# Storing the gradients of two neighbouring heads as one transfer with 16 KiB rows, in the second pass of an attention backward kernel

## The chip, the cores and the metric

The kernel runs on one core of one Trainium2 chip. The metric is the device time of one execution in microseconds; the program does the whole computation, forward and backward, in one launch. A core has TensorE (PE; its weight loads are shown apart, as PEld), VectorE (DVE), ScalarE (ACT), GpSimd (POOL) and SyncE (SP), which run their own instruction streams in order and wait for each other by semaphores. Sixteen DMA engines move data between the main memory (HBM) and the on-chip memory (SBUF, 128 partitions). A transfer that SP issues goes through hardware queue q1; one that GpSimd issues goes through software queue q0.

## The reference

One decode step (one query per sequence, a cache of 4096 keys) of a block with attention and an MLP, and the gradients of all its inputs. What is computed for the cache, cut to what matters (B = 2 sequences, H = 32 heads, Sk = 4096, Dh = 128, all in bfloat16):

```python
q = (layernorm(x) @ wq).reshape(B, 1, H, Dh).transpose(0, 2, 1, 3)
scores = einsum("bhqd,bhkd->bhqk", q, k_cache) * (Dh ** -0.5)
p = softmax(scores)
o = einsum("bhqk,bhkd->bhqd", p, v_cache)
h = x + o.transpose(0, 2, 1, 3).reshape(B, 1, H * Dh) @ wo
out = h + relu(layernorm(h) @ w1) @ w2
# returned: out and the gradients of x, k_cache, v_cache, wq, wo, w1, w2
```

For one query the gradients of the caches are outer products. With `go` the gradient at `o` of a head, `dp = v_cache @ go` and `gs = p * (dp - dot)`, where `dot` is one number for each head: gV = p (outer) go and gK = gs (outer) q, each 4096 x 128 for every one of the 64 pairs (sequence, head). So 64 MB of keys and 64 MB of values are read, the values a second time in most cases, and 128 MB of gradients are written.

## The kernel before

**Layout.** A head's cache of 1 MB is one tile of 128 partitions: partition p holds the 32 neighbouring rows 32p to 32p+31, 8 KiB that are contiguous in HBM (`natural`, L498). A gradient tile has the same layout, so each 1 MB transfer has 128 rows of 8 KiB.

**First pass** (`p1_iter`, L508). It reads K and V of all 64 pairs in order and makes the probabilities P (kept in `P_bf`, L233) and what the middle needs. The middle (`middle_gen`, L860) gives `go` for groups of heads.

**Second pass** (`p2_iter`, L971). In the order `turns` (L455) it goes through the pairs once more. For pair j it reads V again (tile W; six of each sequence's V tiles are kept from the first pass), transposes it on TensorE in four groups (`pair_transpose`, L474: four transposes into PSUM tile t_ps, then ScalarE copies to t_sb) and multiplies with go (`pair_matvec`, L490) into `dp`. Two matmuls spread the rows go and q over all partitions of the same PSUM bank (L985), ScalarE scales them into `rb` (L990), and GpSimd doubles P into `pp` (L992; VectorE's outer product reads each factor twice side by side). VectorE makes the gV tile in two halves of 2048 elements (`outer_half`, L951). In the next turn `p2_gs` (L959) makes the scaled gradient `gsp`, doubled, from `dp`, and VectorE makes gK in two halves. Each tile is stored when its second half is there (L1004, L1025).

The plan (L1243 to L1249) starts the second pass beside the first: pairs 0 to 13 of it run there, and store through GpSimd. Pairs 14 to 63 and the last gK run alone (`i is None`), and store through SP. There ScalarE makes eight of a gV's 32 blocks (L1024, `act`) for pairs up to j = 32, with factors `pa` that GpSimd casts (L996). Work of the middle and of the end (`fin_gen`, L1106: the weight gradients `ot`, stored through GpSimd at L1101; `gx_gen`, L1140: the gradient of x) runs in between, by a given rate a step.

**Buffers.** Thirteen 1 MB homes in the pool `big` (8 KiB a partition) carry tags: `ld` for loads, `g` for gradient tiles, `f` for `ot`, `q` for the end's loads. `take` and `give` (L112, L128) hand them around first in, first out; `share` (L141) sets how many each tag should own. When the second pass is alone, a pool `big1` adds two homes and the shares are ld = 10, of which six hold kept V tiles, and g = 5. Later the six tiles of the weights wo come free one after the other (`late`, L1317), three for g and three for q. Loads wait in a list (`pump`, L1268) and are issued on SP, in the program's order with the stores, as soon as a home of `ld` is free; SP waits in that order.

Of the kernel before, what the change touches and what calls it, by code (L numbers as in the profile page):

```python
# [7 lines left out]
FP32 = mybir.dt.float32  # L8
BF16 = mybir.dt.bfloat16
ALU = mybir.AluOpType  # L10
# [5 lines left out]
def kernel(  # L16
# [89 lines left out]
    owned = dict(free)  # L106
    wanted = {}
    pools = [big] * NBIG
    home_of = {}
    given_at = {}  # L110

    def take(tag, shape, name):  # L112
        assert free[tag] > 0, (tag, name)
        free[tag] -= 1
        k = homes[tag].pop(0)
        t = pools[k].tile(shape, BF16, tag=tag_of.get(k, f"big{k}"), bufs=1, name=name)
        home_of[id(t)] = (tag, k, t)
        return t

    def goes_to(tag):  # L120

        if owned[tag] > wanted.get(tag, len(pools)):
            for other in homes:
                if owned[other] < wanted.get(other, 0):
                    return other
        return tag

    def give(t, to=None):  # L128
        tag, k, _ = home_of.pop(id(t))
        to = to or goes_to(tag)  # L130
        owned[tag] -= 1
        owned[to] += 1
        free[to] += 1
        homes[to].append(k)
        given_at[k] = step[0]
# [14 lines left out]
                    d[tag] -= 1  # L150
                    d[to] += 1

    tag_of = {}

    def more_home(tag, pool, name=None):
        if name:
            tag_of[len(pools)] = name
        homes[tag].append(len(pools))
        pools.append(pool)
        free[tag] += 1  # L160
        owned[tag] += 1
# [70 lines left out]
    NPS = 52  # L232
    P_bf = cols.tile([128, NPS, NSC], BF16)  # L233
    P_free = list(range(NPS))
    P_slot = {}
    ga = cols.tile([128, B, NF], FP32)
    nc.vector.memset(ga[:], 0.0)
# [127 lines left out]
    qc = pkp.tile([128, H, B], BF16)  # L365
    WH = 6
    NWO = -(-H // WH)
    wo_t = [wop.tile([128, NSC * 128], BF16, tag=f"wo{t}", bufs=1, name="wo_t") for t in range(NWO)]

    def wo_of(h, c0, c1):  # L370
        return wo_t[h // WH][:, (h % WH) * D + c0:(h % WH) * D + c1]
# [73 lines left out]
    pairs = [(b, h) for b in range(B) for h in range(H)]  # L445
    NP1 = len(pairs)
    KEPT = (6, 6)
    GROUPS = []
    for b in range(B):
        first = H - KEPT[b]  # L450
# [497 lines left out]
    def pairs_view(t):  # L948
        return t.rearrange("p s (a two) -> p s a two", two=2)

    def outer_half(dst, row, colp, k, short=0):  # L951
        n = HALF - short
        sl = slice(k * HALF, k * HALF + n)
        nc.vector.tensor_tensor(  # L954
            out=pairs_view(dst[:, sl, :]),
            in0=row.rearrange("p (a two) -> p a two", two=2)[:, None, :, :].to_broadcast([128, n, 64, 2]),
            in1=colp[:, sl, None, :].to_broadcast([128, n, 64, 2]), op=ALU.mult)
# [10 lines left out]
        P_free.append(P_slot.pop((bp, hp)))  # L968
        return gsp

    def p2_iter(j, busy, act=0, store=None):  # L971
        store = store or nc.gpsimd

        c = S2[j] if j < NP1 else None
        p = S2.get(j - 1)
        if p is not None:
            bp, hp = turns[j - 1]
            gsp = p2_gs(j - 1)
        if c is not None:
            b, h = turns[j]  # L980
            go = gom[:, h, b, :, :]

            bank = pst([128, 512], FP32, "sps", "dp_ps")
            for k, col in enumerate((goc, qsc)):
                nc.tensor.matmul(bank[:, 128 + k * 128:256 + k * 128],  # L985
                                 lhsT=col[:, h, b:b + 1].to_broadcast([128, 128]), rhs=ident_bf[:],
                                 start=True, stop=True)
            c["dp"] = bank[:, 0:NSC]
            rb = mats.tile([128, 256], BF16, tag="rb", bufs=3, name="rb")
            nc.scalar.activation(out=rb[:], in_=bank[:, 128:384], func=ACT.Copy, scale=rt[:, b, h:h + 1])  # L990
            pp = small.tile([128, NSC, 2], BF16, tag="pp", bufs=2, name="pp")
            nc.gpsimd.tensor_copy(out=pp[:], in_=P_bf[:, P_slot[(b, h)], :, None].to_broadcast([128, NSC, 2]))  # L992
            c.update(rb=rb, pp=pp)
            if act:
                pa = small.tile([128, act], FP32, tag="pa", bufs=2, name="pa")
                nc.gpsimd.tensor_copy(out=pa[:], in_=P_bf[:, P_slot[(b, h)], NSC - act:NSC])  # L996
            c["T0"] = pair_transpose(c["W"], 0, busy=busy)
        if p is not None:
            gK = take("g", [128, NSC, 128], "gK")
            outer_half(gK, p["rb"][:, 128:256], gsp, 0)  # L1000
        yield
        if p is not None:
            outer_half(gK, p["rb"][:, 128:256], gsp, 1)
            store.dma_start(out=natural(out_2, bp, hp), in_=gK[:])  # L1004
            give(gK)
            del S2[j - 1]
        yield
        if c is None:
            return
        c["T1"] = pair_transpose(c["W"], 1, busy=busy)  # L1010
        pair_matvec(c["dp"], c.pop("T0"), 0, go)
        yield
        c["T2"] = pair_transpose(c["W"], 2, busy=busy)
        pair_matvec(c["dp"], c.pop("T1"), 1, go)
        yield
        c["T3"] = pair_transpose(c["W"], 3, busy=busy)
        give(c["W"], "g" if j < H and j != 1 and owned["g"] < 3 else None)
        pair_matvec(c["dp"], c.pop("T2"), 2, go)
        gV = take("g", [128, NSC, 128], "gV")
        outer_half(gV, c["rb"][:, 0:128], c["pp"], 0)  # L1020
        yield
        outer_half(gV, c["rb"][:, 0:128], c["pp"], 1, act)
        for k in range(act):
            nc.scalar.activation(out=gV[:, NSC - act + k, :], in_=c["rb"][:, 0:128], func=ACT.Copy, scale=pa[:, k:k + 1])  # L1024
        store.dma_start(out=natural(out_3, b, h), in_=gV[:])  # L1025
        give(gV)
        yield


    def p2_tail(j):  # L1030

        p = S2[j]
        bp, hp = turns[j]
        gsp = p2_gs(j)
        yield
        gK = take("g", [128, NSC, 128], "gK")
        outer_half(gK, p["rb"][:, 128:256], gsp, 0)
        yield
        outer_half(gK, p["rb"][:, 128:256], gsp, 1)
        nc.gpsimd.dma_start(out=natural(out_2, bp, hp), in_=gK[:])  # L1040
        give(gK)
        del S2[j]
        yield
# [254 lines left out]
    def p2_step():  # L1298
        nonlocal g2
        try:  # L1300
            next(g2)
        except StopIteration:
            g2 = None

    for n, (i, j) in enumerate(plan):
        all_go = all(("go", B - 1, h) in done for h in range(H))
        if i is None and plan[n - 1][0] is not None:
            pkp.release()
            big1 = tc.alloc_tile_pool(name="big1", bufs=1)
            for _ in range(2):  # L1310
                more_home("ld", big1)
            share(ld=KEPT[1] + 4, g=5)
        if ("w1", B - 1) in done:
            for t in range(NWO):
                if t not in late and all(("go", B - 1, h) in done for h in range(t * WH, min(H, (t + 1) * WH))) and \
                        (t < NWO - 1 or all_go):
                    late[t] = ("g", "g", "g", "q", "q", "q")[len(late)]  # L1317
                    more_home(late[t], wop, f"wo{t}")
        lq, ll, lg = [sum(v == tag for v in late.values()) for tag in ("q", "ld", "g")]
        if fin is not None and not bg2 and not bg3:  # L1320
            share(ld=4, g=12 + 6 * (lq > 0))
        elif fin is not None and j >= H + KEPT[1] - 1:
            share(ld=4 + ll, g=7 + lg, f=3, q=2 + lq)
        if j is not None:
            while g2 is not None:
                p2_step()
            if j < NP1:
                bg_until(("go", *turns[j]))
            if i is not None and n + 1 < len(plan) and plan[n + 1][1] is None:
                g2 = p2_whole(j)  # L1330
            else:
                g2 = p2_iter(j, 0, 8 if i is None and j <= H else 0, nc.sync if i is None else None)
        if i is None and ("w1", 1) in done and fin is None:
            wts.release()
            fin = tc.alloc_tile_pool(name="fin", bufs=1)
            big2 = tc.alloc_tile_pool(name="big2", bufs=1)
            more_home("f", big2)
            banks.update(sps=[2, 3], o=[4, 5, 6])
            bg2.append(("fin", fin_gen(fin)))
            bg3.append(("gx", gx_gen(fin)))  # L1340
        if i == 12:
# [9 lines left out]
        if i is None:  # L1351
            mixed[0] = False
            spread[0] = 2
            at_k[0] = 1
            k = 0
            while g2 is not None:
                p2_step()
                pump()
                slot[0] = int(k in ((1, 3, 5) if j <= H else (1, 4)))
                k += 1  # L1360
                bg_step(0, rate)
                bg_step(1, RATE2 * (0.4 if spreading[0] else 1.0))
                bg_step(2, RATE3)
            continue
# [64 lines left out]
```

## Time and profile before

| | |
|---|---|
| median of three runs | 890.82 us (889.17 to 891.23) |
| profiled execution | 887.9 us |
| its span, first to last instruction | 886.1 us |
| busy: PE, PEld | 736.0 us, 614.3 us |
| busy: DVE, ACT, POOL | 690.8 us, 478.0 us, 155.8 us |
| moved by DMA | 361.87 MB, mean 408 GB/s over the span |
| second pass alone | from about 456 us to the end |
| last instruction of a compute engine | ends at about 868 us |

Engines work side by side, so the rows do not add up. A slice line of the profile divides the span into 40 equal slices and gives tenths of busy time; a stretch's row gives busy microseconds of each engine with the number of instructions, the clock that TensorE was granted, the mean share of the 16 DMA engines and what they moved. A wait row names the engine that waits, the line, who ended the wait, the total, the number of times and the longest. An issue row gives the number of transfers, their size and the median time from issue to landing.

### The profile page before, as it was taken

How to read it: one execution, taken by the hardware profiler on the slowest of the kernel's cores; microseconds unless marked ns; L12 is line 12 of the kernel's file. 1: busy time of each engine (PE TensorE's matmuls, PEld its weight loads, DVE VectorE, ACT ScalarE, POOL GpSimd, SP SyncE). 2: the span in 40 equal slices, each digit the busy share in tenths (PEclk: the TensorE clock that was granted, in tenths of full speed). 3: DMA queues.
4: the chain of work that ended last, by engine and by line, in shares of the span. 5: the costliest groups of instructions: out<-in, count | busy, mean ns of one | idle time of the engine just before them, and what ended most of it. 6: DMA issues, size and time to landing. Idle time of an engine off the chain costs nothing.

```text
span 886.1 us, 24945 instructions
## 1 busy us (share of the span) xinstructions
PE 736.0 (83%) x10215; PEld 614.3 (69%) x10215; DVE 690.8 (78%) x1309; ACT 478.0 (54%) x1241; POOL 155.8 (18%) x264
## 2 busy tenths in 40 slices
PE   4999899999999998878967777878878896937971
PEld 4888788888888887777856666656757665625640
DVE  2666698877888887777868797678989998799750
ACT  1344343344565655455546777767756555526661
POOL 1344344343210000010011110011010001101200
PEclk9999899999999999999996556555666756556565
DMA  9999999999889999999999999999999999999995
GB/s 377 425 417 417 421 413 420 424 423 416 323 298 392 424 424 426 423 424 426 423 405 415 422 425 425 425 422 412 419 425 414 419 419 427 415 426 421 408 425 229
DMA packets 56115, 361.87 MB, mean 408 GB/s; under 512 B 5712, under 2 KB 11728, under 8 KB 15296
## 3 DMA queue, kind: packets, MB, share of 16 engines
q1 hardware_dynamic: 49096, 317.04, 86.5%
q0 software_dynamic: 6864, 43.22, 11.7%
q8 instruction: 80, 1.31, 0.5%
q14 instruction: 35, 0.29, 0.1%
q10 hardware_dynamic: 40, 0.01, 0.0%
HBM read 211.11 MB, written 149.13 MB: 407 GB/s over the span
## 4 chain that ended last, share of the span: by engine, by line
PE 38%; DMA 21%; DVE 19%; issue 12%; ACT 8%; SPq 0%; POOL 0%; ACTq 0%; POOLq 0%; DVEq 0%
PE t_ps L482 17%; DMA Vt<-in_A_v_cache_dram 10%; PE m_ps L516 9%; DVE gK L954 5%; DVE gV L954 5%; DMA out_dram<-gK 4%; DVE rows L711 4%; DVE pk L523 3%; ACT t_sb L487 3%; PE s_ps L495 3%; PE u_ps L545 3%; DMA out_dram<-ot 2%; ACT gV L1024 2%; DMA wqs<-in_A_wq_dram 2%; PE dp_ps L495 2%
## 5 line engine op out<-in xcount | busy, mean ns | idle before, releaser
L487 ACT COPY t_sb<-t_ps 128x512 f32<-128x512 f32 x479 | 274.2, 587 | 208.7 <-PE t_ps L482 205.4
L495 PEld LDWEIGHTS <-t_sb 128*128 128x128 bf16 x4096 | 177.7, 102 | 57.2 <-ACT t_sb L487 28.8
L482 PE MATMUL t_ps<-ident_f,Wt 128*128 128x128 f32 x832 | 192.6, 381 | 9.0 <-DMA Wt<-in_A_v_cache_dram 8.4
L523 DVE TENSOR_TENSOR pk<-Kt,ep 128x2048 bf16<-128x2048 bf16 x128 | 156.3, 1222 | 39.7 <-ACT ep L570 31.4
L516 PE MATMUL m_ps<-pk,Vt 128*128 128x129 bf16 x2048 | 170.6, 222 | 13.5 <-DMA Vt<-in_A_v_cache_dram 13.5
L482 PEld LDWEIGHTS t_ps<-ident_f,Wt 128*128 128x128 f32 x832 | 134.7, 197 | 38.1 <-issue 30.6
L482 PE MATMUL t_ps<-ident_f,Kt 128*128 128x128 f32 x1024 | 157.0, 286 | 4.1 <-DMA Kt<-in_A_k_cache_dram 3.4
L954 DVE TENSOR_TENSOR gK<-rb,gsp 128x2048 bf16<-128x2048 bf16 x128 | 153.2, 1222 | 8.9 <-DMA out_dram<-gV 7.1
L516 PEld LDWEIGHTS <-Vt 128*128 128x128 bf16 x2048 | 124.5, 98 | 43.5 <-issue 27.7
L954 DVE TENSOR_TENSOR gV<-rb,pp 128x2048 bf16<-128x2048 bf16 (+1 forms) x128 | 143.3, 1140 | 2.7 <-DMA out_dram<-gK 2.6
L482 PEld LDWEIGHTS t_ps<-ident_f,Kt 128*128 128x128 f32 x1024 | 113.5, 145 | 7.8 <-ACT t_sb L487 3.8
L533 POOL COPY pk<-ep 128x16 bf16<-128x16 bf16 x78 | 83.2, 1069 | 155.6 <-ACT ep L570 80.5
L495 PE MATMUL dp_ps<-gom,t_sb 128*128 128x2 bf16 x2048 | 95.3, 168 | 16.9 <-ACT t_sb L487 16.0
L495 PE MATMUL s_ps<-qm,t_sb 128*128 128x2 bf16 x2048 | 87.6, 164 | 1.3 <-DVE t_sb L485 1.3
L1099 ACT CAST ot<-o_ps 128x512 bf16<-128x512 f32 (+3 forms) x152 | 66.8, 493 | 5.1 <-DMA out_dram<-ot 3.0
L992 POOL COPY pp<-P_bf 128x64 bf16<-128x64 bf16 x64 | 30.3, 478 | 163.6 <-DVE gV L954 152.0
L630 ACT CAST wo_t<-m_ps 128x128 bf16<-128x128 f32 x55 | 14.6, 266 | 78.1 <-PE m_ps L516 77.9
L711 DVE CUSTOM_DVE_ANT_0 rows<-wqs,gqr 128x1024 bf16<-128x1024 bf16 x40 | 48.9, 1221 | 9.6 <-DMA wqs<-in_A_wq_dram 9.4
L990 ACT ACTIVATE rb<-dp_ps,rt 128x256 bf16<-128x256 f32 x64 | 30.3, 473 | 44.2 <-PE dp_ps L985 43.3
L711 DVE CUSTOM_DVE_ANT_0 rows<-wo_t,rows 128x640 bf16<-128x640 bf16 x64 | 52.4, 819 | 0.8 <-ACT rows L688 0.4
L1024 ACT ACTIVATE gV<-rb,pa 128x128 bf16<-128x128 bf16 x152 | 46.5, 392 | 6.4 <-DMA out_dram<-gV 6.4
L711 DVE CUSTOM_DVE_ANT_0 rows<-w_t,rows 128x640 bf16<-128x640 bf16 (+2 forms) x53 | 42.3, 799 | 2.9 <-ACT rows L688 2.7
(205 smaller groups left out, 690.3 us busy)
## 6 DMA issues: line engine op xcount, KB each, us to landing
Kt<-in_A_k_cache_dram SPq DMA_DIRECT2D x64, 1024.0 KB, 18.7
Vt<-in_A_v_cache_dram SPq DMA_DIRECT2D x64, 1024.0 KB, 15.1
Wt<-in_A_v_cache_dram SPq DMA_DIRECT2D x52, 1024.0 KB, 16.4
out_dram<-gK SPq DMA_DIRECT2D x51, 1024.0 KB, 16.7
out_dram<-gV SPq DMA_DIRECT2D x50, 1024.0 KB, 15.1
out_dram<-gV POOLq DMA_DIRECT2D x14, 1024.0 KB, 10.4
out_dram<-gK POOLq DMA_DIRECT2D x13, 1024.0 KB, 10.3
out_dram<-ot POOLq DMA_DIRECT2D x6, 960.0 KB, 10.0
```

What stands on the lines that cost most here:

```text
L482: nc.tensor.transpose(t_ps[:, j, :], natf[:, 2 * cc:2 * cc + 2, :].rearrange("p c k -> p (c k)"), ident_f[:])
L487: nc.scalar.copy(out=t_sb[:], in_=t_ps[:])
L495: nc.tensor.matmul(dst[:, sc:sc + 2], lhsT=v[:, j, :, par], rhs=vecs[:, par, :], start=(par == 0), stop=(par == 1))
L516: nc.tensor.matmul(r["m"][:, 0:129], lhsT=r["V"][:, sc, :], rhs=r["pk"][sc // HALF][:, sc % HALF, 0:129], start=(sc == 0), stop=(sc == NSC ...
L523: nc.vector.tensor_tensor(out=p["pk"][k][:, :, 0:128].rearrange("p s (a two) -> p s a two", two=2), in0=p["K"][:, sl, :].rearrange("p s (a ...
L533: nc.gpsimd.tensor_copy(out=col, in_=e)
L711: nc.vector.tensor_tensor_reduce(out=junk[0:kc, 0:width], in0=in0, in1=in1, scale=1.0, scalar=0.0, op0=ALU.mult, op1=ALU.add, accum_out=acc)
L954: nc.vector.tensor_tensor(out=pairs_view(dst[:, sl, :]), in0=row.rearrange("p (a two) -> p a two", two=2)[:, None, :, :].to_broadcast([128 ...
L990: nc.scalar.activation(out=rb[:], in_=bank[:, 128:384], func=ACT.Copy, scale=rt[:, b, h:h + 1])
L992: nc.gpsimd.tensor_copy(out=pp[:], in_=P_bf[:, P_slot[(b, h)], :, None].to_broadcast([128, NSC, 2]))
L1024: nc.scalar.activation(out=gV[:, NSC - act + k, :], in_=c["rb"][:, 0:128], func=ACT.Copy, scale=pa[:, k:k + 1])
L1099: nc.scalar.copy(out=ot[0:kp, k, n0:n0 + nn], in_=o_ps[0:kp, 0:nn])
```

## The change

When the second pass is alone, two neighbouring heads (h even, h + 1) are handled as one couple in two 2 MB tiles, called twins. Viewed as one array, the gradients of two heads are contiguous 2 MB; partition p now holds 64 neighbouring rows, 16 KiB, so partitions 0 to 63 hold the first head and 64 to 127 the second (`natural2`). The 16 KiB rows are the change's unit of storing.

- `p2_two` replaces two calls of `p2_iter`. Its inner `head(k)` issues the four `pair_transpose` and the first three `pair_matvec` of head h + k, over six steps. Four matmuls spread go and q of the two heads over 64 partitions each, one `rb` serves both. `halves` moves a head's factors from 128 partitions with 32 columns to 64 partitions with 64 columns, by matmuls with the selector `sel`; it is done for P at once, and for the scaled gradients of both heads in the next couple (`last_gk`), where VectorE doubles them from PSUM. ScalarE copies P doubled (`pp`) and the last 16 factors (`pa`), in place of GpSimd.
- gV of a couple takes three instructions of 2048 elements on VectorE and 16 blocks on ScalarE in two sets of eight, up to j = 32, and four on VectorE after that. Its store is issued when all of it is there. gK takes four on VectorE, in the next couple's first steps; its store is one transfer too, but for the last couple, where it is two halves with 8 KiB rows.
- Buffers: the homes lie in one tile `big_t`, so that homes 3 and 4, and 10 and 11, can be joined to twins when both have been given back. The third twin is the pool `big1`, the fourth is tiles 2 and 3 of the weights wo, when they come free. The remaining homes of g go to ld. The tiles 0, 1 and 4 of wo go to q, tile 5 to f, and the last shares are ld = 5, f = 4, q = 5.
- The steps of a couple are as many as those of two pairs, and the background work gets its turns at the same steps.

```diff
@@ take, give, share
+    big_t = big.tile([128, NBIG, NSC * 128], BF16, name="big_t")
+    place = {k: big_t[:, k, :] for k in range(NBIG)}
...
+    def park(k):
+        parked.add(k)
+        pair = twin[k]
+        if parked.issuperset(pair[0:2]):
+            twos.append(pair[2])
...
     def give(t, to=None):
         tag, k, _ = home_of.pop(id(t))
+        if k in twin:
+            owned[tag] -= 1
+            park(k)
+            return
...
+    TWINS = (3, 10)
...
+    def halves(dst, cols_of):
+        for c in range(2):
+            for par in range(2):
+                nc.tensor.matmul(dst[64 * c:64 * c + 64, par * NSC:(par + 1) * NSC], lhsT=sel[:, par, :],
+                                 rhs=cols_of[c], start=True, stop=True)
+
+    def natural2(cache, b, h):
+        return cache[b, h:h + 2].rearrange("h (p sc) d -> (h p) sc d", sc=2 * NSC)
+
+    def gs_of(j):
+        p = S2[j]
+        bp, hp = turns[j]
+        pair_matvec(p["dp"], p.pop("T3"), 3, gom[:, hp, bp, :, :])
+        nc.vector.scalar_tensor_tensor(out=ALONE["gs"][:, hp % 2, :], in0=p["dp"], scalar=negdot[:, hp, bp:bp + 1],
+                                       in1=P_bf[:, P_slot[(bp, hp)], :], op0=ALU.add, op1=ALU.mult)
...
+    def last_gk(split=False):
+        p = last[0]
+        gs_of(p["j"] + 1)
+        yield
+        t = S2[p["j"] + 1]["bank"][:, 128:128 + 2 * NSC]
+        halves(t, [ALONE["gs"][:, c, :] for c in range(2)])
+        gsp = pp_t[:].rearrange("p a s two -> p (a s) two")
+        nc.vector.tensor_copy(out=gsp, in_=t[:, :, None].to_broadcast([128, 2 * NSC, 2]))
...
+        yield
+        gK = twos.pop(0)
+        out = natural2(out_2, p["b"], p["h"])
+        for k in range(4):
+            outer_half(gK, p["rb"][:, 128:256], gsp, k)
+            if split and k % 2:
+                sl = slice((k - 1) * HALF, (k + 1) * HALF)
+                nc.sync.dma_start(out=out[:, sl, :], in_=gK[:, sl, :])
+            if k < 3:
+                yield
+        if not split:
+            nc.sync.dma_start(out=out, in_=gK[:])
+        twos.append(gK)
+        yield
...
+    def p2_two(j, act):
...
+        next(before, None)
+        bank = pst([128, 512], FP32, "sps", "dp_ps")
+        S2[j].update(bank=bank, dp=bank[:, 0:NSC])
+        for k, col in enumerate((goc, qsc)):
+            for c in range(2):
+                nc.tensor.matmul(bank[64 * c:64 * c + 64, 128 + k * 128:256 + k * 128],
+                                 lhsT=col[:, h + c, b:b + 1].to_broadcast([128, 64]), rhs=ident_bf[:],
+                                 start=True, stop=True)
+        halves(bank[:, 384:384 + 2 * NSC], [P_bf[:, P_slot[(b, h + c)], :] for c in range(2)])
+        rb = mats.tile([128, 256], BF16, tag="rb", bufs=3, name="rb")
+        nc.scalar.activation(out=rb[:], in_=bank[:, 128:384], func=ACT.Copy, scale=ALONE["rt"][:, b, h // 2:h // 2 + 1])
...
+        first = head(0)
+        next(first)
+        nc.scalar.copy(out=pp[:], in_=bank[:, 384:384 + 2 * NSC, None].to_broadcast([128, 2 * NSC, 2]))
+        if act:
+            nc.scalar.copy(out=pa[:], in_=bank[:, 384 + 2 * NSC - act:384 + 2 * NSC])
...
+        for _ in range(5):
+            next(before, None)
+            next(first)
+            yield
+        for _ in before:
+            pass
+        gV.append(twos.pop(0))
+        by_act(0, act // 2)
+        yield
+        gs_of(j)
+        second = head(1)
+        next(second)
+        yield
+        for k in range(4):
+            next(second)
+            if k < 3 or not act:
+                outer_half(gV[0], rb[:, 0:128], pp, k)
+            yield
+        by_act(act // 2, act)
+        yield
+        next(second)
+        nc.sync.dma_start(out=natural2(out_3, b, h), in_=gV[0])
+        twos.append(gV[0])
...
@@ the loop over the plan
-            for _ in range(2):
-                more_home("ld", big1)
-            share(ld=KEPT[1] + 4, g=5)
+            twos.append(big1.tile([128, 2 * NSC, 128], BF16, name="two_t"))
...
-        if fin is not None and not bg2 and not bg3:
-            share(ld=4, g=12 + 6 * (lq > 0))
-        elif fin is not None and j >= H + KEPT[1] - 1:
-            share(ld=4 + ll, g=7 + lg, f=3, q=2 + lq)
+        if fin is not None and j >= H + KEPT[1] - 1:
+            share(ld=5, f=3 + lf, q=2 + lq)
...
+            if i is None and j < NP1:
+                bg_until(("go", *turns[j + 1]))
+                g2 = p2_two(j, HALF if j <= H else 0)
+            elif i is None:
+                g2 = last_gk(True)
```

## The prediction

> **What bounds the kernel now.** First I read the slices of the whole span and the two big queues, to see which resource is never idle.
>
> ```profile
> DMA  9999999999889999999999999999999999999995
> DMA packets 56115, 361.87 MB, mean 408 GB/s; under 512 B 5712, under 2 KB 11728, under 8 KB 15296
> q1 hardware_dynamic: 49096, 317.04, 86.5%
> q0 software_dynamic: 6864, 43.22, 11.7%
> q8 instruction: 80, 1.31, 0.5%
> ```
>
> The 16 DMA engines are full from the first slice to the last but one, except slices 11 and 12, which lie before the changed part. Then the table of busy time by stretch (span, PE, PEld, DVE, ACT, POOL, PE clock, DMA share, GB/s), over the second pass alone (456 us on) and its end:
>
> ```profile
> 480.00:520.00 40.00, 31.44 (x361) 27.39 (x360) 34.95 (x64) 29.95 (x81) 6.68 (x12) 0.51 1.01 422
> 600.00:640.00 40.00, 34.71 (x343) 28.11 (x341) 38.13 (x66) 27.55 (x67) 3.42 (x8) 0.59 1.01 414
> 640.00:680.00 40.00, 33.10 (x339) 26.52 (x338) 35.64 (x62) 25.29 (x55) 5.57 (x10) 0.60 1.01 425
> 456.00:860.00 404.00, 313.67 (x3116) 245.34 (x3115) 341.27 (x565) 254.83 (x618) 45.86 (x88) 0.59 1.01 420
> 872.00:876.00 4.00, 0.00 (x0) 0.00 (x0) 0.00 (x0) 0.00 (x0) 0.00 (x0) 0.50 0.77 316
> 876.00:880.00 4.00, 0.00 (x0) 0.00 (x0) 0.00 (x0) 0.00 (x0) 0.00 (x0) 0.50 0.18 76
> 880.00:884.00 4.00, 0.00 (x0) 0.00 (x0) 0.00 (x0) 0.00 (x0) 0.00 (x0) 0.50 0.06 27
> ```
>
> DMA is at 1.01 in every stretch of the pass (over 1 because a packet's recorded time overlaps the next one's by about 1%). VectorE, with 341 of 404 us, is the next engine, TensorE with 314 the one after. The last rows show the end: no compute after 868 us, and 0.06 is one engine of sixteen. One DMA engine is behind the others and ends the span alone. So the time moves only if each DMA engine has less to do, or if a DMA engine runs out of work. Last, the waits of VectorE and ScalarE in the pass, and the issues:
>
> ```profile
> DVE gsp L965 <- PE dp_ps L495: 21.4, 12, 7.6
> DVE gK L954 <- DMA out_dram<-gV: 7.1, 4, 4.5
> ACT gV L1024 <- DMA out_dram<-gV: 6.4, 1, 6.4
> out_dram<-gK SPq DMA_DIRECT2D x51, 1024.0 KB, 16.7
> out_dram<-gV SPq DMA_DIRECT2D x50, 1024.0 KB, 15.1
> ```
>
> Waits for a buffer are small; a store lands 15 to 17 us after its issue, about 6 MB ahead of it at 420 GB/s. The queue is deep, and compute refills it in time.
>
> **The change, part by part.** Of the 51 gK and 50 gV stores on SP, the first gK (pair 13) stays single. The other 50 pairs make 25 couples: 25 gV stores and 24 gK stores of 2 MB in 16 KiB rows, and the last gK in two halves with 8 KiB rows.
>
> (1) *DMA packets.* The packet records give the price: 1,280 B take 55 ns, 4,096 B 159 ns, 8,192 B 309 ns. The slope is (309-55)/6912 = 0.03675 ns a byte, so the bytes of a row need 301 ns. Packets follow each other after 309/1.01 = 306 ns, so a packet costs 306-301 = 5 ns beside its bytes. A couple's store has 128 packets in place of 256, 8 fewer on each of the 16 engines: 49 x 8 x 5 ns = 1.96 us. Each store also ends with a 4-byte packet per engine (9 ns, 6 of them not overlapped); 100 stores become 51: 49 x 6 ns = 0.29 us. Together -2.25 us on every engine, the late one too. The trace has no 16 KiB data packet. One bound is the slope, as above. The other is q8's instruction fetches, the only 16 KiB packets: 0.5% x 16 x 886 us / 80 = 886 ns each, 275 more than the 612 of two 8 KiB packets, and x 392 that is +108 us. I take the slope, since rows of one kind from 1,280 to 8,192 B lie on it, while the fetches go to another place. The Trainium skill (DMA: Bandwidth & Descriptors, "Why small descriptors are slow") states a fixed overhead of about 3 cycles a packet; with that page's 850 MHz an estimate is 3.5 ns, and 392 of them 1.4 us instead of 1.96. The trace's 5 ns is larger and decides here.
>
> (2) *VectorE.* A couple had four gK halves (1.223 us), with ScalarE's help two full and two short gV halves (1.220, 0.685), and two gsp (0.280): 9.26 us. It gets four gK halves, three gV halves, two scaled-gradient instructions over 32 instead of 64 elements and one copy of 128 from PSUM. The 32-element one is between L618's 0.191 (32 from PSUM) and 0.280; the copy is nearest L563's 0.290 (128 from PSUM). Sum 9.22 to 9.40. For the 15 couples without ScalarE's help it is +0.11 to +0.29 us. All lies under DMA: VectorE has 63 us idle in the 404. Without that cover it would be at most 25 x 0.3 = 7 us.
>
> (3) *ScalarE and GpSimd.* Per couple one rb (0.473) falls away and a copy of 128 (L1099's 0.277) and one of 16 (L535's 0.264) come: +0.07 us. The blocks of gV, 16 a couple, remain. GpSimd loses 50 pp and 19 pa; these stood behind its ot stores, which wait up to 18 us for ScalarE, so compute gets freer: zero while DMA is full.
>
> (4) *TensorE.* rb's four matmuls stay four, with half the columns of weights. Eight `halves` matmuls a couple are new; L390's on the same selector take 0.19 each, so 1.5 us a couple at most, 38 us in all, against 90 us of idle time. Their instructions, 25 x 16 with the weight loads, at 1.31 MB/24945 = 53 B each, are 21 KB, 1.3 more fetches of 886 ns on one engine, less GpSimd's: 0 to +1.1 us if that engine is the late one; I take 0.3.
>
> (5) *The order behind new waits.* The gsp copy waits for TensorE's four `halves` instead of only the last matvec, and four gK halves queue behind it on VectorE; TensorE has the next transposes (1.0 us) ahead of them. I bound it by 0 and 1.5 us a couple; it is on the path only when DMA runs dry. ScalarE's first eight blocks wait for a twin that was last stored a whole couple earlier (about 14 us before); behind that wait stand its copies of t_ps, and TensorE behind those. But at such a moment everything issued after that store, two loads and two couples' stores, is still queued, so DMA loses nothing. On SP a 2 MB gV store waits for the last eight blocks, with the next loads behind it; cover is the queue again.
>
> (6) *Buffers and the seam.* At the start of the pass the kernel before lets VectorE and ScalarE wait until 468 us for a g buffer; the first twin is fresh memory, so the first gV couple is issued at about 472 us, when the single gV was (471.35). Later 2 MB units hold the first head's megabyte back for some 7 us. Issued bytes less moved bytes give the queue before each issue: the lowest points are 1.36 MB at 466.7, 1.45 at 576, 1.31 at 601, 1.43 at 679 and 1.60 at 856. One held megabyte leaves 0.3 MB or more, two would not. Bounds 0 and +10 us; I take 0, since from 560 us on the late engine has 2 to 10 us more work queued than these means say (a store's sixteenth arrival comes that much after its fifteenth).
>
> Sum: -1.96 - 0.29 + 0.3 = -1.95 us against the profiled execution (887.9 us, of which the span is 886.1). The median of the runs shown is 890.8; the same difference gives **888.8 us**. Own range 886.5 to 890.0.
>
> **The rivals.** *A, the packets are not merged or cost as little as half* (the store's rows are cut at 8 KiB, or the 5 ns lie mostly in the shared end of a packet): gain 0.3 to 1.2 us, less the fetches: 890.3. For: no 16 KiB data packet is in the trace. Against: q8 shows that a packet of this size exists.
>
> *B, slower: the twins run the DMA queue dry.* Three twins and three load buffers take the place of five g and four load buffers. A couple's megabyte is held while its neighbour is computed; if both the gK and the gV twin are held at one time, 2.1 MB are missing. At each of the low points of (6), with the seam's group counted once and two at 851 to 856, that is 2.1 - 1.45 = 0.65 MB, 1.55 us at 420 GB/s; six or seven such points are 10 us, less 2: 898.5. It decides as soon as more than 1.4 MB is held at a low point. For: VectorE is busy for 38 of 40 us where the queue is drained (600 to 680 us), and (4) and (5) add to TensorE there. Against: stores of the other kind and loads lie between, and the last engine's backlog is longer.
>
> *C, the late engine catches up*: the single engine's 6 to 8 us at the end come in part from short and foreign packets; with fewer turns it might end 3 us earlier: 885.8. Nothing in the profile shows that it would.
>
> *D, large packets are as slow as q8's*: 890.8 + 108 = 999.
>
> **How the numbers follow.** Forecast 0.50, A 0.17, B 0.25, C 0.06, D 0.02. Of no change the measurement can tell 0.2%, 1.8 us: 889.0 to 892.6. The forecast's range straddles that: 0.42 of its 0.50 is counted as faster, for its own sum lies only just outside, 0.06 as same, 0.02 as slower. A is same. B is slower but for 0.02 same; C is faster, D slower. So faster 0.42 + 0.06 = 0.48, same 0.06 + 0.17 + 0.02 = 0.25, slower 0.02 + 0.23 + 0.02 = 0.27. The range leaves out D, the far side of B and half of C: 885.5 to 897.5.
>
> **What would show it.** q1's packets fall by 49 x 128 + 49 x 16, from 49096 to about 42,040, with 16 KiB ones of about 611 ns; the share stays 1.01 and the rate in full stretches rises from 422-426 to 427-429 GB/s where stores prevail. A share under 1.00 in a stretch after 466 us is B, first at the seam and near 580, 600 and 680. More packets than 42,040 are A. The forecast is wrong if the last compute ends after 872 us with an empty queue, or if the end shows no tail of a single engine.

## The result: 904.45 us, slower by 1.5%

Four runs after the change have a median of 904.45 us (902.35 to 905.66) beside 891.03 us (889.17 to 893.5, four runs) of the kernel before: a ratio of 1.0146, 95% interval 1.0113 to 1.018. The profiled execution took 905.66 us, its span 903.9 us. First the page of the kernel after: the slices, what each slice moved, and the packets by queue.

```profile
DMA  9999999999789999999998999999999999999995
GB/s 378 417 410 413 416 407 418 420 417 400 301 290 406 424 423 421 422 424 420 410 388 358 370 395 428 356 414 421 419 419 409 417 428 425 425 428 427 425 405 220
DMA packets 49058, 361.87 MB, mean 400 GB/s; under 512 B 4928, under 2 KB 10944, under 8 KB 14512
q1 hardware_dynamic: 42040, 317.04, 85.5%
q0 software_dynamic: 6864, 43.22, 11.5%
q8 instruction: 82, 1.34, 0.6%
```

The merge happened: q1 has the 42,040 packets that were forecast, for the same bytes. What was lost stands in the second row: slices 21 to 24 (388, 358, 370, 395) and slice 26 (356). In the row of tenths only slice 22 shows it; GB/s tells what the busy share hides. The stretches of the second pass (same columns as before the change: PE, PEld, DVE, ACT, POOL, clock, DMA share, GB/s) give the places:

```profile
480.00:520.00 40.00, 28.79 (x333) 24.84 (x332) 27.03 (x51) 24.45 (x69) 0.00 (x0) 0.50 0.89 356
560.00:600.00 40.00, 33.40 (x321) 26.36 (x318) 29.86 (x63) 27.95 (x81) 0.53 (x1) 0.54 0.95 380
600.00:640.00 40.00, 34.41 (x340) 27.65 (x340) 33.69 (x68) 30.16 (x85) 1.62 (x3) 0.54 1.01 420
640.00:680.00 40.00, 35.38 (x306) 26.34 (x306) 33.68 (x57) 21.86 (x46) 1.10 (x2) 0.50 1.01 422
894.00:898.00 4.00, 0.00 (x0) 0.00 (x0) 0.00 (x0) 0.00 (x0) 0.00 (x0) 0.50 0.14 58
```

In the second of these stretches the kernel before has this row:

```profile
560.00:600.00 40.00, 31.84 (x276) 23.92 (x277) 27.34 (x60) 28.80 (x80) 3.11 (x9) 0.50 1.01 423
```

Where the kernel before moved 422 GB/s from 480 to 520 us, this one moves 356, and VectorE and ScalarE have less to do there too: 27.0 against 35.0 us and 24.5 against 30.0. From 600 to 680 us nothing is lost. The tail of a few DMA engines at the end is there as it was. The waits that answer to those shown of before are these (engine, tile and line, who ended the wait: total, times, longest):

```profile
ACT two_t L1172 <- DMA out_dram<-two_t: 5.5, 1, 5.5
PE dp_ps L531 <- ACT t_sb L523: 6.0, 3, 5.3
DVE two_t L990 <- DMA out_dram<-two_t: 2.8, 1, 2.8
```

and the issues of the couples' stores (times, KB each, median us to landing):

```profile
out_dram<-big_t SPq DMA_DIRECT2D x27, 2048.0 KB, 19.5
out_dram<-two_t SPq DMA_DIRECT2D x15, 2048.0 KB, 17.0
out_dram<-wo_t SPq DMA_DIRECT2D x7, 2048.0 KB, 24.7
```

Together they are the 49 stores of 2 MB that were forecast.

The three waits fall between 478 and 500 us. What SP issued around them, and ScalarE's instruction, in the timeline (start, length, what, and in brackets the idle time before it and what ended it):

```profile
481.31 0.34 SPq L1196 DMA_DIRECT2D out_dram<-two_t  x1
487.88 0.34 SPq L1104 DMA_DIRECT2D out_dram<-big_t  x1
497.29 0.34 SPq L539 DMA_DIRECT2D big_t<-in_A_v_cache_dram  x1
500.30 0.33 SPq L1196 DMA_DIRECT2D out_dram<-two_t  x1
490.88 1.28 ACT L1172 ACTIVATE two_t<-rb,pa_t 128x128 bf16<-128x128 bf16 x4 [5.45 <-DMA out_dram<-two_t]
```

The second couple's gV blocks want the twin `two_t`, which the first couple's gV has just left in the queue (issued at 481.31). ScalarE stands still until that store has landed; behind it wait its copies of t_ps, behind those TensorE, and SP issues nothing from 488.2 to 497.3. By then the queue is empty: issued bytes less moved bytes are 0.01 MB at 495.9 us.

One more difference lies before the changed part: the load of K 32 is issued at 175.9 us in place of 173.7, and that of K 40 at 241.7 in place of 237.4. The order of instructions in the first pass is the same. K 32 turns out to be the steadier mark of the two: variants of the kernel before that lose no time have it at 173.7 to 174.0, but K 40 anywhere from 236.8 to 239.0 (e14).

### The profile page after: what moved, and what is told of

Read it like the earlier page. It is cut to its first block, busy times and chain, and to the rows that moved or that the text cites. A ratio compares the mean times of both kernels' runs of the same rounds, so it can differ in the third digit from the quotient of the medians.

```text
span 903.9 us, 24996 instructions
## 1 busy us (share of the span) xinstructions
PE 759.4 (84%) x10415; PEld 633.1 (70%) x10415; DVE 690.5 (76%) x1324; ACT 476.3 (53%) x1259; POOL 123.4 (14%) x197
## 3 DMA queue, kind: packets, MB, share of 16 engines
q1 hardware_dynamic: 42040, 317.04, 85.5%
## 4 chain that ended last, share of the span: by engine, by line
PE 34%; DMA 22%; DVE 19%; issue 16%; ACT 5%; SPq 0%; POOL 0%; DVEq 0%; ACTq 0%; POOLq 0%
PE t_ps L518 15%; DMA big_t<-in_A_v_cache_dram 13%; PE m_ps L552 8%; DVE big_t L990 6%; DVE rows L747 4%; DVE pk L559 3%; DMA big_t<-in_A_wq_dram 3%; PE s_ps L531 3%; DMA out_dram<-big_t 2%; ACT t_sb L523 2%; PE u_ps L581 2%; PE o_ps L1265 2%; DVE wo_t L990 2%; DMA big_t<-in_A_k_cache_dram 2%; PE dp_ps L531 1%
## 5 line engine op out<-in xcount | busy, mean ns | idle before, releaser
L518 PE MATMUL t_ps<-ident_f,big_t 128*128 128x128 f32 x2048 | 397.3, 335 | 8.8 <-DMA big_t<-in_A_k_cache_dram 5.9
L518 PEld LDWEIGHTS t_ps<-ident_f,big_t 128*128 128x128 f32 x2048 | 275.9, 170 | 42.4 <-issue 23.7
L559 DVE TENSOR_TENSOR pk<-big_t,ep 128x2048 bf16<-128x2048 bf16 x128 | 156.3, 1222 | 42.0 <-ACT ep L606 33.1
L552 PE MATMUL m_ps<-pk,big_t 128*128 128x129 bf16 x2048 | 171.2, 223 | 16.3 <-DMA big_t<-in_A_v_cache_dram 15.4
L990 DVE TENSOR_TENSOR big_t<-rb,pp_t 128x2048 bf16<-128x2048 bf16 x134 | 159.0, 1219 | 5.9 <-DMA out_dram<-big_t 5.5
L552 PEld LDWEIGHTS <-big_t 128*128 128x128 bf16 x2048 | 124.9, 99 | 47.5 <-issue 28.7
L990 DVE TENSOR_TENSOR two_t<-rb,pp_t 128x2048 bf16<-128x2048 bf16 x56 | 66.1, 1219 | 4.3 <-DMA out_dram<-two_t 4.2
L747 DVE CUSTOM_DVE_ANT_0 rows<-big_t,wo_t 128x1024 bf16<-128x1024 bf16 x40 | 48.7, 1218 | 5.1 <-DMA big_t<-in_A_wq_dram 5.1
L581 PE MATMUL u_ps<-pk,hot 128*32 128x512 bf16 x512 | 40.3, 391 | 0.0
L990 DVE TENSOR_TENSOR big_t<-rb,gsp 128x2048 bf16<-128x2048 bf16 x28 | 34.0, 1220 | 3.9 <-DMA out_dram<-big_t 3.9
```

The source lines that it names most:

```text
L518: nc.tensor.transpose(t_ps[:, j, :], natf[:, 2 * cc:2 * cc + 2, :].rearrange("p c k -> p (c k)"), ident_f[:])
L552: nc.tensor.matmul(r["m"][:, 0:129], lhsT=r["V"][:, sc, :], rhs=r["pk"][sc // HALF][:, sc % HALF, 0:129], start=(sc == 0), stop=(sc == NSC ...
L559: nc.vector.tensor_tensor(out=p["pk"][k][:, :, 0:128].rearrange("p s (a two) -> p s a two", two=2), in0=p["K"][:, sl, :].rearrange("p s (a ...
L581: nc.tensor.matmul(u_bank[0][32 * g:32 * g + H, :], lhsT=hot[:, H - 1 - hr:2 * H - 1 - hr], rhs=r["pk"][k // 4][:, 4 * g:4 * g + 4, 0:128] ...
L747: nc.vector.tensor_tensor_reduce(out=junk[0:kc, 0:width], in0=in0, in1=in1, scale=1.0, scalar=0.0, op0=ALU.mult, op1=ALU.add, accum_out=acc)
L990: nc.vector.tensor_tensor(out=pairs_view(dst[:, sl, :]), in0=row.rearrange("p (a two) -> p a two", two=2)[:, None, :, :].to_broadcast([128 ...
```

## The experiments

**Is the late first pass an accident of one run?** *e1* runs the kernel before once more; nothing is changed.

> The kernel before once more, for the spread of its stages. In the profile shown the 61st key tile was issued at 384.7 us and pair 13's gV at 459.0; in the changed kernel's at 390.1 and 466.7, though the instructions of the first pass are the same there. Theory 1 (the loss lies in the second pass alone, where DMA runs out of work): part or all of these 5 to 8 us is spread between executions, so this run falls anywhere from 384 to 390, and its whole time is 888 to 894. Theory 2 (the change slows the transfers of the first pass too, by the place of the tiles): 384 to 386 again.

It took 888.71 us, with K 32 at 173.9 and K 40 at 236.9. The 61st key tile came at 387.4 us, which by the expectation is theory 1's range, so that mark varies between executions. K 32 does not: the other variants at the addresses of the kernel after (e2 to e4) have it at 176.0 to 176.3. So a delay early in the first pass belongs to the kernel after.

**Large rows or small ones.** *e2* is the kernel after with its 2 MB stores split by rows:

```diff
-            nc.sync.dma_start(out=out, in_=gK[:])
+            for c in range(2):
+                sl = slice(c * NSC, (c + 1) * NSC)
+                nc.sync.dma_start(out=out[:, sl, :], in_=gK[:, sl, :])
```

and so for gV. 

> The changed kernel, but each 2 MB store is issued, at the same place, as two of 1 MB with 8 KiB rows. Theory 1: the larger packets themselves help by the 2 us worked out, so this is 904.5 + 2 = 906 to 907 us, with the same gaps in the transfers. Theory 2 (large rows are slow): 895 us or less.

909.38 us, ratio 1.0209 (1.0173 to 1.0245), later than either case expected. Here the small rows cost about 5 us more, though the two intervals overlap a little; e10 prices them again without the wait at the seam and at the addresses of before.

**Holding less.** *e3* stores the first half of each gV and gK couple as soon as it is made, and the second at the end, each 1 MB with 8 KiB rows.

```diff
-        nc.sync.dma_start(out=natural2(out_3, b, h), in_=gV[0])
+            if k == 1:
+                nc.sync.dma_start(out=natural2(out_3, b, h)[:, 0:NSC, :], in_=gV[0][:, 0:NSC, :])
...
+        nc.sync.dma_start(out=natural2(out_3, b, h)[:, NSC:2 * NSC, :], in_=gV[0][:, NSC:2 * NSC, :])
```

> The changed kernel, but the first half of each gV and gK couple (8 KiB rows, 1 MB) is stored as soon as VectorE has made it, the second half when it is there. Buffers come free in couples as before. Theory 1 with the held megabyte as its cause: the queue no longer runs dry near 580 us, at the seam it does by less; 904.5 + 2 - 4 = 902 to 903 us. If the number of buffers and not the held data is the cause: 906 to 907, as with rows of 8 KiB alone.

900.53 us, ratio 1.0124 (1.0086 to 1.0162), earlier than either case expected. That is well below e2, which has the same rows, but the interval overlaps that of the kernel after. The rate still falls to 358 GB/s from 580 to 600 us, and ScalarE's wait at the seam is still there:

```profile
ACT two_t L1170 <- DMA out_dram<-two_t: 5.7, 1, 5.7
```

**The seam.** The list `twos` is first in, first out, and the twin of homes 10 and 11 joins it behind `two_t`. *e4* puts that twin first:

```diff
-            twos.append(pair[2])
+            twos.insert(0 if pair[0] == TWINS[1] else len(twos), pair[2])
```

> The changed kernel, but the twin of homes 10 and 11 goes to the head of the list when it comes free, so that the second couple's gV takes it and not the first twin, whose store is still under way (in the profile ScalarE waited for it from 485.4 to 490.9 us, and DMA had a share of 0.57 in the 10 us behind that). Theory 1: the wait and most of the gap go: 5 us less, 899 to 900 us. If the gap has another cause, such as the loads that come too late: 903 to 905 us.

898.68 us, ratio 1.009 (1.0056 to 1.0124). ScalarE's wait for a store is gone, and the stretch in which the kernel after had a share of 0.78 and 313 GB/s reads in e4:

```profile
480.00:500.00 20.00, 16.48 (x227) 14.74 (x226) 14.74 (x28) 14.17 (x41) 0.00 (x0) 0.52 1.00 408
```

Its dents at 560 to 600 us stay (365 and 392 GB/s).

**Where the homes lie.** The change adds pp_t (256 bytes a partition) ahead of the pool `big` and takes away pp (256) and pa (64), so every home lies 64 bytes lower, and the homes have become slices of one tile. The unused tile `pad` of 128 bytes shifts them without touching anything else. *e5* gives the kernel before the slices at the old address; *e6* gives it `PAD = 64`; *e7* is the kernel after with `PAD = 192`. *e8* has e7's pad, e4's list and e3's halves together.

```diff
-    PAD = 128
+    PAD = 64
```

> The kernel before, with the after's storage and nothing else of the change: the thirteen homes are slices of one tile big_t, the projection weights slices of wo_all, and pp a slice of pp_t, so `big` starts at the same address as before. No store is merged. It asks why the after's FIRST pass is late (K32's load issued 2.2 us later, K40's 4.3 us). Theory T (one tile makes the framework wait for more than one home, or order them otherwise): K32 at 176, K40 at 241 and the whole at 893 to 895. Theory S (the base address of `big` moved by 64 bytes): no change here, K32 at 173.8, K40 at 237, whole at 890 to 891.

> The kernel before with the unused tile `pad` 64 bytes instead of 128, so that every home lies 64 bytes lower in its partition, as it does in the after, and nothing else. Theory S (address): K32 at 176, K40 at 241, whole 893 to 895 from this alone, the store packets of 8 KiB longer than 309 ns in the median or with more stragglers. Theory T: 890 to 891 and K32 at 173.8.

> The after with `pad` of 192 bytes, so that the homes lie at the addresses that they have in the before. Theory S: the first pass is again that of before (K32 at 173.8, K40 at 237) and the whole falls from 904.5 to 900 to 902. Theory T: 904 to 905, first pass still late.

> The after with three changes together: pad of 192 bytes, the twin of homes 10 and 11 first in the list (it gave 5.8 us), and the first half of every couple of gV and gK stored as soon as it is there, with 8 KiB rows (it gave 3.9 us alone). If the seam's wait, the late halves and the first pass add up: 904.5 - 5.8 - 3.9 - 3 = 892 us, give or take 2. If the seam and the halves repair the same gap: 896 to 898.

The address it is. e5: 889.85 us, 0.9998 (0.9979 to 1.0017). e6: 896.17 us, 1.0057 (1.0024 to 1.0089), for 64 bytes of nothing, a little later than its case. e7: 897.97 us, 1.0085 (1.0056 to 1.0114), some 2 us better than its case. e8: 894.45 us, 1.0041 (1.0024 to 1.0058), between its two cases. e9 below has the same ratio without the halves, so they add nothing that can be seen once the address and the seam are repaired. Why they helped in e3, where ScalarE waited at the seam as before, stays open.

*e11*, *e13* and *e14* are the kernel before with `PAD` 256, 384 and 640, to find the rule.

> The kernel before with `pad` of 256 bytes in place of 128: every home 128 bytes higher. If it is the place of the homes against a multiple of 128 bytes that costs the 5.5 us of e6, this is as before: 890 to 891, 8 KiB packets at a mean of 315 ns and instruction fetches at 940 ns. If only the one address of before is good, or a larger power of two decides, it is slower: 893 to 897, fetches near 1020 ns.

> The kernel before with every home 256 bytes higher (`pad` 384). If the place of a home against multiples of 256 bytes decides: as before, 890 to 891, with fetches at 940 ns. If multiples of 512 or more decide: 893 to 896, fetches near 1000 ns.

> The kernel before with every home 512 bytes higher (`pad` 640). If multiples of 256 or 512 bytes decide: 890 to 891 and fetches at 940 ns. If only this one address is good, 893 to 896.

e11: 895.07 us, 1.0047 (1.0028 to 1.0065). e13: 889.64 us, 0.9995 (0.9975 to 1.0016). e14: 891.1 us, 0.9998 (0.9974 to 1.0021). In a table worked out from the packet records (8 KiB packets on q1 that began between 50 and 200 us, where the queue is full; times of packets and fetches in ns):

```
homes against before   median  mean    longer than 309 ns   fetch (q8), mean   K 32 issued   ratio
before                 309     311.3    2%                  943                173.7         1
-64 bytes (e6)         312     315.3   69%                  1018               176.4         1.0057
+128 bytes (e11)       309     314.0   41%                  1003               175.4         1.0047
+256 bytes (e13)       309     311.3    2%                  939                174.0         0.9995
+512 bytes (e14)       309     311.1    2%                  944                173.8         0.9998
the kernel after       312     315.2   69%                  1017               175.9         1.0146
after, PAD 192 (e7)    309     311.6    2%                  938                174.0         1.0085
```

The kernel after has e6's packets, and with 64 bytes more it has those of before. A shift by 256 or 512 bytes costs nothing, one by 64 or 128 does. All packets counted in the table are loads: no store is issued before 200 us. Where stores run, less is seen of it: of the 8 KiB packets that GpSimd's stores sent from 300 to 450 us 13% are longer than 309 ns in e6, 4% before; of those on q1 from 700 to 850 us, where most of SP's bytes are stores, 8% against 5%.

The Trainium skill has a rule with this boundary (DMA: Bandwidth & Descriptors, "How a descriptor splits into AXI transactions"): a transfer that does not start on a multiple of 256 bytes begins at the boundary below it and fetches the bytes before its start for nothing. The traces agree on the boundary, if the homes of before lie on one: the starts then lie 192 bytes behind it in e6 and 128 in e11, a ratio of 1.5, and the means rise by 4.0 and 2.7 ns, also about 1.5. They do not settle the mechanism, for the rule speaks of bytes that are fetched, and the packets lengthened here belong to loads, which write the shifted tiles. The page gives no time for it; here it is 0.5 to 0.6% of the whole.

**What remains.** *e9* is the kernel after with `PAD` 192 and e4's list, 16 KiB rows kept. *e10* is e9 with e2's split rows.

> The after with two repairs, 16 KiB rows kept: `pad` of 192 bytes (homes at the addresses of before) and the twin of homes 10 and 11 first in the list (no wait at the seam). Theory H (held bytes: a 2 MB store issued late runs the queue dry between 500 and 600 us whatever came before): the stretch 500 to 600 still moves 39.5 to 40.2 MB against 42.4 of before, and the whole is 892 to 893. Theory L (lag: TensorE and VectorE set the pace there, so the queue runs dry by as much as the compute came late into that stretch, and the late first pass and the seam were that lag): 41.3 MB or more, and the whole is 888 to 890, at or below before.

> As e9, but each 2 MB store issued as two of 1 MB with 8 KiB rows at the same place. It prices the packets alone, now without a wait at the seam and at the addresses of before. By the prediction's part 1 (7056 packets fewer at 5 ns on 16 engines) it is 2.2 us slower than e9; by the comparison of e2 with the after it is about 5 us slower. If larger rows gain only where the queue is full, 1 to 2 us.

e9: 894.47 us, ratio 1.0039 (1.0019 to 1.0058). e10: 893.86 us, 1.0047 (1.0031 to 1.0062). From 500 to 600 us e9 moved 40.0 MB, inside theory H's range; the kernel before moved 42.4. L, which wanted 41.3 MB or more, has fallen. The whole is later than H's 892 to 893 too. e10 was expected 1 to 5 us behind e9; the ratios differ by 0.7 us and the medians by 0.6 us the other way, so no price of the packets can be read from the pair. The stretches of e9, then one each of before and e10:

```profile
500.00:520.00 20.00, 12.34 (x154) 10.47 (x153) 17.39 (x31) 15.53 (x44) 0.00 (x0) 0.67 1.01 410
520.00:540.00 20.00, 16.13 (x171) 14.07 (x168) 19.05 (x37) 13.47 (x37) 0.00 (x0) 0.59 1.01 409
560.00:580.00 20.00, 17.31 (x149) 13.18 (x149) 12.79 (x26) 14.14 (x40) 0.53 (x1) 0.50 0.88 340
700.00:850.00 150.00, 128.24 (x1152) 94.69 (x1151) 134.06 (x198) 85.49 (x197) 5.17 (x9) 0.53 1.01 427
```

```profile
500.00:600.00 100.00, 74.81 (x728) 61.63 (x727) 80.13 (x156) 73.82 (x202) 11.23 (x25) 0.53 1.01 424
```

```profile
700.00:850.00 150.00, 122.33 (x1150) 90.67 (x1149) 133.39 (x197) 83.41 (x193) 5.16 (x9) 0.57 1.01 425
```

To see whether compute was late or the queue short, both are put against the same progress: ScalarE copies t_ps to t_sb four times for each pair, so the copies, counted from the last one back, say how far the pass is. Between copy n and n-8 (two pairs), the bytes issued less the bytes moved:

```
            before                            e9
copy   reached at  mean MB  lowest      reached at  mean MB  lowest
184    490.7 us    3.85     3.05        490.4 us    2.31     1.09
176    506.6       3.72     3.02        506.5       2.48     1.27
168    520.0       4.52     3.72        518.2       3.46     2.44
152    549.6       3.87     2.46        551.2       2.02     0.71
144    567.2       2.80     1.50        568.9       2.34     0.16
```

By these copies compute is on time to within 2 us, and the queue holds 0.5 to 1.9 MB less, at its lowest points 1.3 to 2.0 MB less. What is missing can be counted at the same copies by kind of transfer: e9 had issued 1.6 to 2.0 MB less in stores than the kernel before, the held couples, and also 1.0 to 1.2 MB less in loads, which is one load. (The queue is not shorter by all of it, since less had been moved as well.) The nine homes that are left for loads hold the six kept V tiles and so give three load buffers; the kernel before has four. So two things make the queue thinner, and no run of the changed kernel moves one without the other. e8 doesn't separate them: its halves brought the stores at most 0.5 MB further than in e10, which has the same rows.

The queue need not be empty for the rate to fall: from 500 to 540 us, with 1.3 to 2.4 MB left at the lowest, the share is 1.01 and the rate 410, and the 8 KiB packets on q1 from 500 to 600 us took 346 ns in the mean (311 before). Why they take longer isn't shown. The amount in the queue alone doesn't do it: the kernel before, with 1.5 MB left at its lowest point between 560 and 600 us, moved 423 GB/s there in packets of 311 ns. What SP waits for from 480 to 600 us shows both from the other side. Before:

```profile
SPq L1004 <- DVE gK L954: 27.9, 15, 3.4
SPq L503 <- PE t_ps L482: 24.3, 13, 4.1
```

and e9:

```profile
SPq L539 <- PE t_ps L518: 61.3, 13, 8.0
SPq L1104 <- DVE big_t L990: 14.2, 4, 6.2
```

Before, SP stood mostly before stores that came one after the other. Now it stands for up to 8 us before a load whose home is still being read, with no store of the couple ready to fill the gap, and whatever is ready behind that load waits too.

*e12* holds stores in the kernel before: there, in the second pass alone, the first of two pairs' gV and gK waits for the second pair's, each 1 MB.

```diff
-            store.dma_start(out=natural(out_2, bp, hp), in_=gK[:])
-            give(gK)
+            store_two("gK", j > J0 and (j - 1 - J0) % 2 == 0, natural(out_2, bp, hp), gK)
...
+    def store_two(key, wait, out, t):
+        if wait:
+            held[key] = (out, t)
+            return
+        for o, x in ([held.pop(key)] if key in held else []) + [(out, t)]:
+            nc.sync.dma_start(out=o, in_=x[:])
+            give(x)
```

> The kernel before, with its 8 KiB rows, its compute order and its homes, but in the second pass alone the gV and the gK store of the first pair of every two are issued only together with the second pair's, as 1 MB each: the holding of the after without its large rows, its couples and its seam. Theory H (held bytes run the queue dry between 480 and 600 us): about a megabyte or more less stands in the queue there, 500 to 600 us moves 39.5 to 41 MB in place of 42.4, and the whole is 893 to 895. If holding costs nothing (all that remained of the loss lay in the couples' other order of work): 890 to 891.

896.51 us, ratio 1.0059 (1.004 to 1.0078), later than its cases, and 40.4 MB from 500 to 600 us. So holding costs in that kernel. But it isn't the same loss in the same place. The held tiles also keep homes: VectorE waits 14.1 us for stores from 440 to 620 us in place of 9.7. Counted in copies, compute is 4 us late in this trace before the first store is held, and 10 us late from copy 160 on; loads are on time. From copy 184 to 168 the queue is about as deep as before, not thinner as was expected; the rate falls before that (338 and 314 GB/s in the two 10 us from 470 us on) and at 560 to 580 us (359). So e12 shows that holding can cost as much as the remaining 4 us, waits for homes included. It doesn't show how the 4 us of e9 and e10 divide between held stores and the missing load buffer.

## Why the prediction was wrong

The forecast of 888.8 us and its range missed; the rival B, the slower one, came nearest. Of the four places that it named for a share under 1.00 the seam and 560 to 600 us came (0.89 and 0.95); from 600 to 680 us the share stayed at 1.01. Three steps failed: the cover of part (5), the zero of part (6), and the address, which no part had. The ratios, taken as parts of 891 us, give the balance; a difference of two of them is uncertain by some 0.3% (3 us):

```
couples with 8 KiB rows, address and seam repaired (e10)   1.0047            +4.2 us
rows of 16 KiB (e9 against e10)                            1.0039  -0.0008   -0.7
the seam's wait (e7 against e9)                            1.0085  +0.0046   +4.1
homes 64 bytes lower (after against e7)                    1.0146  +0.0061   +5.4
```

The two repairs nearly add up: the seam alone takes the ratio from 1.0146 to 1.009, the address alone to 1.0085, both to 1.0039.

*Part (1), the packets: right in their number and length; the gain isn't shown.* The 16 KiB packet took 611 ns, as the slope said, and 42,040 packets were left. From 700 to 850 us, where the queue is deep, e9 moves 427 GB/s and e10 425, 0.5%, in one trace each; the forecast 2.25 us of some 400 is 0.56%. Over the whole the 0.7 us can be told neither from zero nor from 2.25. e2's 5 us was not the price of the packets alone. The additional packets there also lie at the bad address; how much that explains stays open. The other bound of the 16 KiB packet used fetches of 886 ns, from a rounded share; the records give 943 ns. That changes nothing in the choice.

*Parts (2) to (4): right in that they cost nothing that shows.* VectorE is busy for 690.5 us (690.8 before), ScalarE for 476.3 (478.0; 1.8 more was forecast), GpSimd for 123.4 (155.8), TensorE for 759.4 (736.0, inside the bound of 38 more); q8 has two fetches more.

*Part (5), the order behind new waits: its bound held (the doubling copy waited 21.1 us for TensorE over the whole pass, 18 times), its cover did not: the first step that failed.* "At such a moment everything issued after that store, two loads and two couples' stores, is still queued" assumed a list of three twins in turn. At the start only two were in it, and the second couple was handed the one just stored. Counted in t_sb copies as above, compute was 3.0 us behind the kernel before at copy 196 and 9.9 us at copy 188, two pairs on.

*Part (6), buffers and the seam: the second step that failed.* "The first gV couple is issued at about 472 us": it was 481.3, and still 475.4 with the address repaired (e7), since a second head's work stands before it. "One held megabyte leaves 0.3 MB or more": at the same copies e9 had issued not 1 but 1.6 to 2.0 MB less in stores, since gK of the first head waits for its neighbour's dot products too, and one load less besides. The loss of a load buffer stands in rival B's count of buffers, but had no term. The sum also took the loss to begin at an empty queue, while in e9 the rate was 410 GB/s with 1.3 MB or more left. The depth of the queue was read too high already under the bounds of the kernel before: "about 6 MB ahead" came from the time to landing, while issued less moved bytes are 3.0 to 4.7 MB in the mean of each 20 us from 480 to 600 us.

The value taken, 0 of 0 to +10, should have been some 8 (4.2 and, for the seam's wait of part (5), 4.1). Rival B's 10 us is close to that, but partly by luck: its sum needed six or seven dry points, and e9 has one with a share clearly under 1.00 (0.2 MB left at 575 us; near 601 and 679 us it keeps 1.2 and 1.6 MB at the lowest, the kernel before 1.3 and 1.5), and 4.1 us are the wait for a twin, which B doesn't have. The sentence against it, that the late engine's backlog would cover, was wrong: the share was 0.88 from 560 to 580 us. How the 4.2 us divide between held stores and the load buffer stays open.

*No part had the address: the third step, a term put at nothing without a reason.* The change's storage was read for its sizes and users, and what a shorter `small` does to everything behind it was given no term: 5.4 us, the largest one, and its lengthened packets lie in the first pass, which the change doesn't touch.

No version of the change that was tried beats the kernel before. Couples only after 620 us, where the queue is deep, might save 0.5% of some 270 us, an estimate of 1.3 us by the rates above; this wasn't tried, and it is below what these runs can tell.

## What to carry to other kernels

Where DMA sets the time, don't cost a larger store by its packets alone: ask what stands in the queue at its lowest points while the store's second half is still being computed, and count the load buffers that the larger tiles take as well. When a change adds or drops a small tile, work out by how much the big tiles behind it move, and pad them back to the same place modulo 256 bytes before anything else is measured. A list of buffers that is first in, first out goes wrong at its start: follow the first three takes by hand.

## What the runs showed of the hardware that was not expected

A shift of the transferred tiles by 64 bytes lengthened 69% of the 8 KiB load packets between 50 and 200 us, by 9 ns in the mean over these, and the program by 0.57%; a shift by 256 bytes did nothing. Instruction fetches, which have no part in those tiles, grew from 943 to 1018 ns beside it. A DMA share of 1.01 went with 409 GB/s in e9 and with 427 GB/s later in the same run, so a full share is no proof of the full rate.
